# Falling rows of the second batch's short chunk: loaded row by row into two halves of a tile, with one on-chip copy in place of two

## The chip, the cores and the metric

The kernel runs on one core of a Trainium2 chip. The core has four compute engines that work side by side: TensorE (PE, matrix products; its weight loads are listed as PEld), VectorE (DVE), ScalarE (ACT) and GpSimd (POOL). SyncE (SP) computes nothing here; it issues transfers, and 16 DMA engines carry them out. The metric is the device time of one execution in microseconds (us), the median of several runs.

## The reference

The input x has 8 batches of 3008 rows of 256 numbers. The reference takes the real part of a two-dimensional Fourier transform of each batch and sends every row through a gated layer of 1536 hidden units:

```python
X = np.fft.fft(x, axis=1)
X = np.fft.fft(X, axis=2)
x = X.real.reshape(24064, 256)
g = x @ w_gate
silu = g * (1.0 / (1.0 + np.exp(-g)))
out = (silu * (x @ w_val)) @ w_out
```

## The kernel before

The Fourier transform is done by matrix products with tables of cosines and sines. Because of its symmetries the rows of a batch are first added and subtracted against one another ("folded"): a row that rises through the batch meets a row that falls through it. Each batch is loaded in two chunks: a long one, tile XA (128 partitions), and a short one, tile XC, of NCR = 60 rows. XC is laid out as partitions x 8 groups x 2 rows x 256: groups 0 to 3 hold the rising rows, groups 4 to 7 the falling ones, and each load brings two neighbouring rows side by side (2 KB), so the third index is the row's parity. Odd batches lie in partitions 64 to 123. Where two batches share a fold, they do so by their halves of the tile; the second batch (b = 1) is folded alone, in one pass over all 128 partitions, and for that its other parity has to stand in partitions 0 to 59.

`load_c` (L152) gives the list of loads of a short chunk. For the second batch it has 22 entries: 15 rising loads (L160; 4 partitions each, 32 KB), 4 falling loads (L162; 60 partitions, 120 KB each), one row for the middle (L164), and the two copies within XC (L158; 240 KB each): the first brings the rising rows' parity 0 from partitions 64 to 123 down to 0 to 59 (as parity 1), the second the falling rows' parity 1 (as parity 0). `fold_steps` (L171) makes the fold on POOL; its first operation is L178 (SDf from XC or XA), then L179, L182, L185 and so on. The partitions 60 to 63 and 124 to 127, which no load writes, are cleared once (L566) by two transfers from a tile of zeros; the zeros are a POOL memset (L563, on the space of Af), and `row_signs` (L345, L346, two small POOL operations) stands between that memset and the clears.

All loads, on-chip copies and output stores of the main part are issued by SP, so they stand in one queue, in program order. Around the change this queue holds: clears, C loads and copies of the second batch, its A loads (L148: 16 of 64 KB; L150: 4 of 256 KB), output stores (L1609), C loads of the third batch (L160, L162), and more stores.

The 24064 rows pass in tiles of 512 columns. For a tile PE makes g and v (L1335), ACT and DVE make from them the gated products (es L1470, sp L1447 and L1519, sv L1522 on ACT; sg L1451, sv L1538, hp L1549 on DVE), POOL makes hm from a pair's sv (L1546), PE multiplies by the last weights (o, L1597), ACT copies o to ev (L1603), and SP stores ev (L1609). There are two sv buffers, three for ev and two for es.

The order of all this after the prologue is made by a list scheduler when the program is built (`Sched`, L1130): each operation is entered by `S.add` with an engine, a duration, what it reads and writes, and for a load its share of the ring (`ring`) and its latency; `S.run` (L1995) starts from a time at which each engine comes free, and gives each engine its sequence. `run_loads` (L1658) enters the loads. What the scheduler is told of a load thus alters the order on every engine. `before` (L1893 to L1898) hangs small jobs on numbered units of the work; L1874 and L1875 are memsets of one of them (`halve_tables`).

Other lines that the steps touch: L356 (DVE) and L352 (POOL) prepare angles in the prologue, L677 to L679 (POOL) fold the first batch, L1818 (POOL) scales weights, L1969 issues Wo, the last weights, from POOL's own queue; L385 issued the weights before it. L660 and L634 are ACT operations of the prologue, L1373 (DVE) the product hp of the first, narrower tiles.

Of the kernel before, what the change touches and what calls it, by code (L numbers as in the profile page):

```python
# [31 lines left out]
def kernel(  # L32
# [8 lines left out]
    nc = tc.nc  # L41
    B, M, D = x.shape
    Dff = moe_w_gate.shape[1]
    P = 128
# [3 lines left out]
    R = M // 4  # L48
# [17 lines left out]
    NCR = GH - P  # L66
# [37 lines left out]
    zero = const.tile([P, 1], F32, name="zero")  # L104
# [6 lines left out]
    Z0 = const.tile([P, 2, 3, P], BF16, name="Z0")  # L111
# [5 lines left out]
    XC = const.tile([P, 8, 2, D], F32, name="XC")  # L117
# [14 lines left out]
    LC, NC_ = 4, NCR // 4  # L132

    def up_block(b, j, n):
        return rows_at(b, 2 * j - 1, [[2 * D, n], [R * D, 4], [1, 2 * D]])

    def rows_at(b, row, ap):
        return bass.AP(tensor=x.tensor, offset=(b * M + row) * D, ap=ap)

    def down_set(b, a, j, L, n):  # L140

        return rows_at(b, R * (a + 1) - 2 * j, [[2 * L * D, n], [-2 * D, L], [1, 2 * D]])

    JA, JC = P - LA + 1, GH - LC + 1
# [7 lines left out]
    def load_c(b, q):  # L152

        X3 = XC.rearrange("p a q d -> p a (q d)")
        p0 = 64 * (b % 2)
        pm = p0 + NCR
        r = slice(p0, p0 + NCR)
        half = [lambda s=s: q.dma_start(out=XC[0:NCR, 4 * s:4 * s + 4, 1 - s], in_=XC[r, 4 * s:4 * s + 4, s])  # L158
                for s in range(2)]
        return ([lambda h=h: q.dma_start(out=X3[p0 + LC * h:p0 + LC * (h + 1), 0:4, :],  # L160
                                         in_=up_block(b, JC - LC * h, LC)) for h in range(NC_)] +
                [lambda a=a: q.dma_start(out=X3[r, 4 + a, :], in_=down_set(b, a, JC, LC, NC_))  # L162
                 for a in range(4)] +
                [lambda: q.dma_start(out=XC[pm:pm + 1, 0:4, 1],  # L164
                                     in_=rows_at(b, 0, [[R * D, 1], [R * D, 4], [1, D]]))] +
                (half if b == 1 else []))

    def fold_steps(eng, X, CE, BB, q, r):  # L171
        tt = eng.tensor_tensor
# [74 lines left out]
    q = nc.sync  # L247
# [3 lines left out]
    zeros = Af.rearrange("p a b d -> p (a b d)")[:, 0:D]  # L251
# [51 lines left out]
    def col(name, n=1, dt=F32):  # L303
        small[name] = tp.tile([P, n], dt, name=name)
        return small[name]
# [17 lines left out]
    half, pc, inside = col("half"), col("pc"), col("inside")  # L323
# [20 lines left out]
    def row_signs():  # L344
        pts(sgo, pc, scalar1=float(NCR), scalar2=-2.0, op0=Alu.is_equal, op1=Alu.mult)  # L345
        pts(sgo, sgo, scalar1=1.0, scalar2=sgn, op0=Alu.add, op1=Alu.mult)  # L346
# [30 lines left out]
    def load_w(first, only=(0, 1)):  # L377
        for i, src in ((0, moe_w_gate), (1, moe_w_val)):
            if i not in only:
                continue  # L380
            w_ = src.rearrange("(no p) f -> p no f", p=P)
            if first:
                nc.gpsimd.dma_start(out=W0[i], in_=w_[:, :, 0:T])
            else:
                nc.gpsimd.dma_start(out=Wraw[i][:, :, 0:Dff - T], in_=w_[:, :, T:Dff])  # L385
# [11 lines left out]
                        in_=rows_at(0, 0, [[2 * R * D, 2], [R * D, 2], [1, D]]))  # L397
    pts(putC, putC, scalar1=pcol, scalar2=1.0, op0=Alu.is_equal, op1=Alu.mult)
    nc.gpsimd.memset(EOf[:, 1, :, P:P + 1], 0.0)
    nc.gpsimd.memset(sel[0:1, :], 1.0)  # L400
    nc.gpsimd.memset(Z0, 0.0)
    load_w(1, (0,))


# [71 lines left out]
    def set_cols(ps, tab, a):  # L476
        if a % 2:
            return (ps[:, 0:2 * GH + 2].rearrange("p (t n) -> p t n", t=2),
                    tab[:, 0:2 * NCE].rearrange("p (t n) -> p t n", t=2)[:, :, 0:GH + 1])
        return ps[:, 0:NCE], tab[:, 0:NCE]  # L480
# [7 lines left out]
    def folded_c(eo):  # L488
        for a in range(2):
            for q in range(2):  # L490
                dst, rhs = set_cols(acc[eo][q], Tab[:, 1, q, eo], a)
                nc.tensor.matmul(dst, EB[:, eo, a, q, :], rhs, start=False, stop=a == 1, skip_group_check=True)
# [64 lines left out]
    X3c = XC.rearrange("p a q d -> p (a q d)")  # L557
# [2 lines left out]
    heads(nc.gpsimd, hd[:, 0], hd[:, 1], CEa)  # L560
    heads(nc.gpsimd, SC[:, 0, 0, :, 0:1], SC[:, 0, 1, :, 0:1], CEc)
    nc.gpsimd.tensor_copy(EOA[:, 0, :, :, P:P + 1], SA[:, 0, :, :, 0:1])
    nc.gpsimd.memset(zeros, 0.0)  # L563
    row_signs()
    for hi in range(2):
        q.dma_start(out=X3c[64 * hi + NCR:64 * hi + 64, :].rearrange("p (c d) -> p c d", d=D),  # L566
                    in_=zeros[64 * hi + NCR:64 * hi + 64].unsqueeze(1).to_broadcast([64 - NCR, 16, D]))
    ptile, qtile = {}, {}

    def pq_tiles(t):  # L570
# [87 lines left out]
    first_tile = {(b, part): tile_of(b * H + part * 2 * G) for b, part in jobs}  # L658
    for k in range(2):
        nc.scalar.activation(BBc[:, :, 1, k, 0:1], SC[:, 0, 1 - k, :, 0:1], AF.Copy, scale=(nsgn, sgn)[k])  # L660
    folded_c(0)
    transform(0, 0, (0,), acc)
    for k in range(2):
# [673 lines left out]
    S = Sched()  # L1337
# [320 lines left out]
    def run_loads(n):  # L1658
        for what, k, fn in loads[:n]:
            up = k < (NA if what[0] == "A" else NC_)  # L1660
            r, w, us, ring = [], [((what[0],), k)], 0.4 if up else 0.62, 0.57 if up or what[0] == "C" else 1.14
            if what == ("A", 1):
                r = [(("C",), NC_ + 6)]
            if what[1] == 1:
                us, ring = 0.6, (0.6 if up else 0.9) if what[0] == "A" else 0.9 if up else 0.7
            if what == ("C", 1) and k > NC_ + 4:
                s = k - NC_ - 5
                r, w = [(("C",), j) for j in (range(NC_, NC_ + 4) if s else range(NC_))], [(("C",), k)]
            S.add("SP", us, fn, r=r, w=w, after=[(("A",), "pre" if k > 15 else "preW")] if what == ("A", 1) else [],
                  lat=2.5, ring=ring)  # L1670
        del loads[:n]
# [4 lines left out]
    def fold_step(what, i, unit):  # L1676
        kind, b = what
        q, j = (1, i) if what == ("C", 1) else divmod(i, 6)
        if i == 0:
            run_loads(max((k + 1 for k, (w_, _, _) in enumerate(loads) if w_ == what), default=0))  # L1680
# [27 lines left out]
    def load_next(what):  # L1708
        kind, b = what
        if kind == "A":  # L1710
            if b + 1 < B:
                loads.extend((("A", b + 1), k, fn) for k, fn in enumerate(load_a(b + 1, nc.sync)))
        else:
            b = b // 2 * 2 + 2
            if b < B:
                loads.extend((("C", b), k, fn) for k, fn in enumerate(load_c(b, nc.sync) + load_c(b + 1, nc.sync)))
# [173 lines left out]
    def odd_op(i):  # L1890
# [4 lines left out]
              7: [lambda: sine_op(0), rows_op], 8: [lambda: sine_op(1)], 9: [weigh_op],  # L1895
              13: [lambda: odd_op(0)], 14: [lambda: odd_op(1)], 15: [lambda: odd_op(2)], 16: [lambda: odd_op(3)],
              17: [lambda: S.add("POOL", 0.8, halve_tables, w=[(("Tab",), "z")])],
              6: []}  # L1898
    before.setdefault(SIGN_AT, []).append(signed_op)

    def row_width(t):
# [43 lines left out]
    for i, u in enumerate(units):  # L1945
# [4 lines left out]
        if i == 1:  # L1950
            loads.extend((("C", 1), k, fn) for k, fn in enumerate(load_c(1, nc.sync)))
        if i == A1_LOAD:
            loads[0:0] = ((("A", 1), k, fn) for k, fn in enumerate(load_a(1, nc.sync)))
        run_loads(LOADS if i < 20 else LOADS_LATER)
        if i in ROW_PE:
            row_op(ROW_PE[i])
# [7 lines left out]
        if i == RESCALE:  # L1964
            state["scaled"] = True
            S.add("ACT", 1.3, lambda: nc.scalar.activation(Wm[:, 1], Wm[:, 1], AF.Copy, scale=-0.5),
                  r=[(("Wm",), (fc, 1)) for fc in range(3)], w=[(("Wm",), 1)])
        if i == 2:
            S.add("POOL", 1.06, lambda: nc.gpsimd.dma_start(out=Wo, in_=moe_w_out.rearrange("(f p) d -> p f d", p=P)),  # L1969
                  w=[(("Wo",), 0)], lat=12.0)  # L1970
# [21 lines left out]
    part_b(prev)  # L1992
    owork = OWork(prev[0], ((psG, "g"), (psV, "v"), (psO, "o")))
    owork.run(len(owork.steps))
    S.run({'DVE': 1.2, 'ACT': 0.9, 'POOL': 4.7, 'PE': 0.0})  # L1995


# [28 lines left out]
```

## Time and profile before

| | us |
|---|---|
| median of 3 runs (604.05, 604.25, 605.38) | 604.25 |
| the profiled execution | 605.04 |
| its span in the profile | 603.2 |
| PE, DVE, ACT, POOL busy | 594.7, 573.2, 562.7, 510.5 |
| zeros' memset on POOL; clears issued | 17.49; 17.82 |
| rising, falling, middle loads of the second batch's C issued from | 19.36, 29.21, 34.68 |
| the two copies within XC issued | 37.84, 39.43 |
| XA's first load; folds of C and of A begin | 40.41; 44.17, 60.33 |

Times in a row of the profile's timeline are a start, counted from the beginning of the span, and a length. A row that stands for several instructions ("x15") runs from the first's start to the last's end. In square brackets stands how long the engine was idle before it and what released it. A row of SP is the issue of a transfer, not the transfer. Busy shares say how full an engine is over the whole span, not which of them sets the end; the chain of work that ended last, also by engine, says that. In the tables by stretches an engine that is busy for the whole length of the stretch has no slack in it.

### The profile page before, as it was taken

How to read it: one execution, taken by the hardware profiler on the slowest of the kernel's cores; microseconds unless marked ns; L12 is line 12 of the kernel's file. 1: busy time of each engine (PE TensorE's matmuls, PEld its weight loads, DVE VectorE, ACT ScalarE, POOL GpSimd, SP SyncE). 2: the span in 40 equal slices, each digit the busy share in tenths (PEclk: the TensorE clock that was granted, in tenths of full speed). 3: DMA queues.
4: the chain of work that ended last, by engine and by line, in shares of the span. 5: the costliest groups of instructions: out<-in, count | busy, mean ns of one | idle time of the engine just before them, and what ended most of it. 6: DMA issues, size and time to landing. Idle time of an engine off the chain costs nothing.

```text
span 603.2 us, 12562 instructions
## 1 busy us (share of the span) xinstructions
PE 594.7 (99%) x4031; PEld 392.2 (65%) x4031; DVE 573.2 (95%) x1055; ACT 562.7 (93%) x1085; POOL 510.5 (85%) x461
## 2 busy tenths in 40 slices
PE   9999999999999999999999999999999999999997
PEld 6556656665666666666666666666666666666686
DVE  8989999999999999999999999999999999999993
ACT  8899987899998999999999999999999999999994
POOL 8828999999799999998999988887878467687772
PEclk9999999999999999999999999999999999999999
DMA  9777346244716224454145212037211212111112
GB/s 239 125 130 137 106 119 202 80 132 121 177 37 168 80 64 127 110 143 122 48 85 143 62 50 77 18 91 184 63 62 37 62 39 69 38 55 51 54 53 79
DMA packets 50510, 57.90 MB, mean 96 GB/s; under 512 B 7222, under 2 KB 37114, under 8 KB 50444
## 3 DMA queue, kind: packets, MB, share of 16 engines
q1 hardware_dynamic: 47484, 54.22, 33.8%
q0 software_dynamic: 2672, 2.36, 2.7%
q8 instruction: 31, 0.51, 0.3%
q10 hardware_dynamic: 288, 0.52, 0.3%
q14 instruction: 35, 0.29, 0.2%
HBM read 29.43 MB, written 24.65 MB: 90 GB/s over the span
## 4 chain that ended last, share of the span: by engine, by line
PE 91%; ACT 4%; DMA 2%; issue 1%; POOL 1%; SPq 0%; DVE 0%; ACTq 0%; DVEq 0%
PE o L1597 39%; PE g L1335 26%; PE v L1335 19%; PE g L1755 2%; PE o L1755 2%; DMA XA<-in_x_dram 1%; PE v L1597 1%; ACT sv L1522 1%; DMA out_dram<-ev 1%; ACT sp L1447 1%; DMA XC<-in_x_dram 0%; ACT sg L1370 0%; POOL EOA L500 0%; ACT es L1470 0%; ACT v L1408 0%
## 5 line engine op out<-in xcount | busy, mean ns | idle before, releaser
L1546 POOL TENSOR_TENSOR hm<-sv 128x1024 bf16<-128x1024 f32 (+2 forms) x137 | 255.2, 1864 | 53.7 <-ACT sv L1522 27.6
L1538 DVE SCALAR_TENSOR_TENSOR sv<-es,v 128x512 f32<-128x512 f32 (+2 forms) x264 | 175.7, 669 | 6.2 <-PE v L1335 5.2
L1597 PE MATMUL o<-Wo,hm 128*128 128x256 bf16 (+1 forms) x1128 | 164.0, 272 | 0.0
L1549 DVE TENSOR_TENSOR hp<-sp,v 128x512 bf16<-128x512 f32 (+2 forms) x238 | 157.8, 670 | 4.6 <-PE v L1335 3.9
L1597 PE MATMUL o<-Wo,hp 128*128 128x256 bf16 (+1 forms) x1104 | 160.1, 272 | 0.0
L1597 PEld LDWEIGHTS <-hm 128*128 128x128 bf16 (+2 forms) x1140 | 111.7, 98 | 59.0 <-issue 2.2
L1597 PEld LDWEIGHTS <-hp 128*128 128x128 bf16 (+2 forms) x1140 | 111.9, 98 | 56.1 <-issue 1.9
L1522 ACT ACTIVATE sv<-g 128x512 f32<-128x512 f32 (+2 forms) x182 | 121.3, 681 | 3.0 <-PE g L1335 2.7
L1447 ACT ACTIVATE sp<-g 128x512 f32<-128x512 f32 (+2 forms) x182 | 113.2, 627 | 4.7 <-PE g L1335 2.7
L1335 PE MATMUL g<-Pt,Wp 128*128 128x512 bf16 (+2 forms) x288 | 107.8, 374 | 1.0 <-ACT sp L1519 0.7
L1408 ACT ACTIVATE v<-bc,w 128x512 f32<-128x512 bf16 (+2 forms) x146 | 105.7, 726 | 2.0 <-DVE sv L1538 0.9
L1335 PE MATMUL g<-Qt,Wq 128*128 128x512 bf16 (+2 forms) x288 | 105.9, 375 | 0.0
L1335 PE MATMUL v<-Pt,Wp 128*128 128x512 bf16 (+2 forms) x288 | 105.6, 375 | 0.0
L1472 DVE SCALAR_TENSOR_TENSOR es<-bc,w,v 128x512 f32<-128x512 bf16 (+2 forms) x128 | 93.2, 732 | 3.2 <-PE v L1335 0.8
L1470 ACT ACTIVATE es<-v 128x512 f32<-128x512 f32 (+2 forms) x146 | 90.7, 624 | 5.4 <-PE v L1335 2.4
L1335 PEld LDWEIGHTS <-Wp 128*128 128x128 bf16 x576 | 56.3, 98 | 27.4 <-issue 3.0
L1335 PE MATMUL g<-Qt,Wm 128*128 128x512 bf16 (+2 forms) x196 | 73.3, 376 | 0.1
L1451 DVE SCALAR_TENSOR_TENSOR sg<-bc,w,g 128x512 f32<-128x512 bf16 (+2 forms) x92 | 66.2, 722 | 1.4 <-PE g L1335 1.0
L1522 ACT ACTIVATE sv<-sg 128x512 f32<-128x512 f32 (+2 forms) x92 | 64.3, 703 | 1.0 <-DVE sg L1515 0.9
L1335 PE MATMUL v<-Qt,Wm 128*128 128x512 bf16 (+2 forms) x160 | 59.8, 374 | 1.9 <-ACT es L1470 1.2
L1519 ACT ACTIVATE sp<-g 128x512 f32<-128x512 f32 (+2 forms) x92 | 57.1, 620 | 4.8 <-DVE sg L1515 4.6
L1515 DVE SCALAR_TENSOR_TENSOR sg<-sg,g 128x512 f32<-128x512 f32 (+2 forms) x92 | 60.7, 660 | 0.3 <-PE g L1335 0.2
(196 smaller groups left out, 757.1 us busy)
## 6 DMA issues: line engine op xcount, KB each, us to landing
out_dram<-ev SPq DMA_DIRECT2D x96, 128.0 KB
XA<-in_x_dram SPq DMA_DIRECT2D x30, 256.0 KB
XA<-in_x_dram SPq DMA_DIRECT2D x112, 64.0 KB
XC<-in_x_dram SPq DMA_DIRECT2D x32, 120.0 KB
XC<-in_x_dram SPq DMA_DIRECT2D x105, 32.0 KB
bc<-br SPq DMA_DIRECT2D x19, 128.0 KB
St<-Fc SPq DMA_DIRECT2D x12, 128.5 KB
out_dram<-ev SPq DMA_DIRECT2D x12, 120.0 KB
```

Source lines behind the costliest of these rows:

```text
L1335: nc.tensor.matmul(ps[:, :n], Wt[:, gv, fs], src[:, :n], start=start, stop=stop, skip_group_check=True)
L1408: nc.scalar.activation(T_[kv][:, :w], bc[t][:, :w], AF.Copy, scale=w0[:, 1, f:f + 1])
L1447: nc.scalar.activation(sp_to()[:, :w], T_[kg][:, :w], AF.Silu)
L1451: nc.vector.scalar_tensor_tensor(T_[keg][:, :w], bc[t][:, :w], w0[:, 0, f:f + 1], T_[kg][:, :w], op0=Alu.mult, op1=Alu.add)
L1470: nc.scalar.activation(T_[kes][:, :w], T_[kv][:, :w], AF.Copy, scale=2.0 if on_pool(u) > 1 else 1.0)
L1472: nc.vector.scalar_tensor_tensor(T_[kes][:, :w], bc[t][:, :w], w0[:, 1, f:f + 1], T_[kv][:, :w], op0=Alu.mult, op1=Alu.add)
L1515: nc.vector.scalar_tensor_tensor(T_[kgm][:, :w], T_[keg][:, :w], 2.0, T_[kg][:, :w], op0=Alu.mult, op1=Alu.subtract)
L1522: nc.scalar.activation(sv()[:, f % 2, w - 1::-1, 1], T_[kgm if by_dve else kg][:, :w], AF.Silu)
L1538: nc.vector.scalar_tensor_tensor(sv()[:, f % 2, w - 1::-1, 0], T_[kes][:, :w], 2.0, T_[kv][:, :w], op0=Alu.mult, op1=Alu.subtract)
L1546: nc.gpsimd.tensor_tensor(hts_(t)[1][:, f - 1:f + 1, :w], sv()[:, :, :w, 1], sv()[:, :, :w, 0], op=Alu.mult)
L1549: nc.vector.tensor_tensor(hts_(t)[0][:, f, :wp], T_[ksp][:, :wp], T_[kv][:, :wp], op=Alu.mult)
L1597: nc.tensor.matmul(st["ps"][:n, j, :], hts[t][minus][:, f, c:c + n], Wo[:, f, :], start=(f == 0), stop=(f == nF - 1))
```

## The change

The falling rows of the second batch's short chunk are no longer loaded in pairs. Each of the four groups is loaded twice, one row of 1 KB per partition: parity 0 to partitions 64 to 123, parity 1 straight to partitions 0 to 59. So the second copy within XC is gone; the copy of the rising rows stays. The list has 25 entries: the middle row, 15 rising loads, 4 falling loads of parity 0, the copy, 4 falling loads of parity 1. The other batches load as before.

The zeros for the clears are now made by ACT (a copy of a broadcast zero) behind L660, and the clears are issued there. `row_signs` moves earlier on POOL, to where Z0 was cleared, and Z0's memset becomes a job of unit 18. The costs of these loads for the scheduler and the beginnings of POOL and SP are changed with it, and XA's loads now stand behind entry 24 of the list in place of entry 21.

```diff
-        half = [lambda s=s: q.dma_start(out=XC[0:NCR, 4 * s:4 * s + 4, 1 - s], in_=XC[r, 4 * s:4 * s + 4, s])
-                for s in range(2)]
...
+        def down(a, k):
+            q.dma_start(out=XC[0:NCR, 4 + a, 0] if k else XC[r, 4 + a, 0],
+                        in_=rows_at(b, R * (a + 1) - 2 * JC + k, [[2 * LC * D, NC_], [-2 * D, LC], [1, D]]))
+
+        downs = [[lambda a=a, k=k: down(a, k) for a in range(4)] for k in range(2)]
+        return mid + ups + downs[0] + [lambda: q.dma_start(out=XC[0:NCR, 0:4, 1], in_=XC[r, 0:4, 0])] + downs[1]
...
-    nc.gpsimd.memset(Z0, 0.0)
+    row_signs()
     load_w(1, (0,))
...
-    nc.gpsimd.memset(zeros, 0.0)
-    row_signs()
-    for hi in range(2):
-        q.dma_start(out=X3c[64 * hi + NCR:64 * hi + 64, :].rearrange("p (c d) -> p c d", d=D),
-                    in_=zeros[64 * hi + NCR:64 * hi + 64].unsqueeze(1).to_broadcast([64 - NCR, 16, D]))
...
         nc.scalar.activation(BBc[:, :, 1, k, 0:1], SC[:, 0, 1 - k, :, 0:1], AF.Copy, scale=(nsgn, sgn)[k])
+    nc.scalar.copy(zeros, zero.to_broadcast([P, D]))
+    for hi in range(2):
+        q.dma_start(out=X3c[64 * hi + NCR:64 * hi + 64, :].rearrange("p (c d) -> p c d", d=D),
+                    in_=zeros[64 * hi + NCR:64 * hi + 64].unsqueeze(1).to_broadcast([64 - NCR, 16, D]))
...
             if what == ("A", 1):
-                r = [(("C",), NC_ + 6)]
-            if what[1] == 1:
-                us, ring = 0.6, (0.6 if up else 0.9) if what[0] == "A" else 0.9 if up else 0.7
-            if what == ("C", 1) and k > NC_ + 4:
-                s = k - NC_ - 5
-                r, w = [(("C",), j) for j in (range(NC_, NC_ + 4) if s else range(NC_))], [(("C",), k)]
+                r = [(("C",), NC_ + 9)]
+                us, ring = 0.6, 0.6 if up else 0.9
+            if what == ("C", 1):
+                us, ring = (0.6, 0.6) if k <= NC_ else (0.9, 0.9)
+                if k == NC_ + 5:
+                    r = [(("C",), j) for j in range(1, NC_ + 1)]
...
-              6: []}
+              18: [lambda: S.add("POOL", 0.8, lambda: nc.gpsimd.memset(Z0, 0.0), w=[(("Z0",), k) for k in range(2)])]}
...
-    S.run({'DVE': 1.2, 'ACT': 0.9, 'POOL': 4.7, 'PE': 0.0})
+    S.run({'DVE': 1.2, 'ACT': 0.9, 'POOL': 3.5, 'PE': 0.0, 'SP': -2.0})
```

More of the change, by code (lines that the diff above doesn't have):

```diff
@@ L157, in load_c @@
         r = slice(p0, p0 + NCR)
-        half = [lambda s=s: q.dma_start(out=XC[0:NCR, 4 * s:4 * s + 4, 1 - s], in_=XC[r, 4 * s:4 * s + 4, s])
-                for s in range(2)]
[L160 to L166, printed above, removed]
+        ups = [lambda h=h: q.dma_start(out=X3[p0 + LC * h:p0 + LC * (h + 1), 0:4, :],
+                                       in_=up_block(b, JC - LC * h, LC)) for h in range(NC_)]
+        mid = [lambda: q.dma_start(out=XC[pm:pm + 1, 0:4, 1],
+                                   in_=rows_at(b, 0, [[R * D, 1], [R * D, 4], [1, D]]))]
+        if b != 1:
+            return ups + [lambda a=a: q.dma_start(out=X3[r, 4 + a, :], in_=down_set(b, a, JC, LC, NC_))
+                          for a in range(4)] + mid
+        def down(a, k):
[3 more added lines that the diff above has]
+        return mid + ups + downs[0] + [lambda: q.dma_start(out=XC[0:NCR, 0:4, 1], in_=XC[r, 0:4, 0])] + downs[1]
     def fold_steps(eng, X, CE, BB, q, r):
```

## The prediction

> **What bounds the kernel now.** I read the page first (busy shares, chain by engine), then busy time by stretches, then the queue of SP and the rows of POOL, DVE and ACT around the places where PE stands still.
>
> ```profile
> span 603.2 us, 12562 instructions
> PE 594.7 (99%) x4031; PEld 392.2 (65%) x4031; DVE 573.2 (95%) x1055; ACT 562.7 (93%) x1085; POOL 510.5 (85%) x461
> PE 91%; ACT 4%; DMA 2%; issue 1%; POOL 1%; SPq 0%; DVE 0%; ACTq 0%; DVEq 0%
> ```
>
> PE is the bound, so an edit counts by what it adds to, or takes from, the few places where PE waits. By stretches (columns: length; then PE, PEld, DVE, ACT, POOL busy with counts; granted clock, DMA share, GB/s):
>
> ```profile
> 60.00:70.00 10.00, 10.00 (x69) 6.81 (x68) 9.88 (x17) 10.00 (x21) 9.89 (x8) 1.00 0.35 109
> 70.00:82.00 12.00, 10.69 (x72) 6.87 (x71) 10.76 (x18) 10.51 (x21) 11.92 (x13) 1.00 0.39 104
> 82.00:155.00 73.00, 72.26 (x495) 48.03 (x493) 70.17 (x131) 64.36 (x126) 71.33 (x70) 1.00 0.48 132
> ```
>
> Just after the changed loads, at 60 to 70, PE, DVE, ACT and POOL are all full: a delay of one there can't be made up. PE's loss is at 70 to 82. Its place, in PE's, ACT's and the chain's rows:
>
> ```profile
> 79.75 0.38 PE L1335 MATMUL v<-Qt,Wm 128*128 128x512 bf16 x1 [1.20 <-ACT es L1470]
> ...
> 78.61 0.59 ACT L1603 COPY ev<-o 128x512 f32<-128x512 f32 x1 [1.49 <-PE o L1597]
> ...
> 74.48 0.56 SPq L1609
> 75.09 3.37 DMA out_dram<-ev
> ```
>
> The page names o as the releaser of that ACT copy, but the chain names the store issued at 74.48, whose transfer ends at 78.5: the copy waits for an ev buffer. Its contents were written at 60.73, and the store left 13.8 us later because SP's queue was full of loads. PE loses here 1.63 (gaps of 1.36 and 0.27 between 77.9 and 80.2). The changed loads stand in this queue:
>
> ```profile
> 17.82 1.50 SPq L566 DMA_DIRECT2D XC<-Af  x2
> 19.36 9.69 SPq L160 DMA_DIRECT2D XC<-in_x_dram  x15
> 29.21 5.29 SPq L162 DMA_DIRECT2D XC<-in_x_dram  x4
> 34.68 0.65 SPq L164 DMA_DIRECT2D XC<-in_x_dram  x1
> 37.84 2.47 SPq L158 DMA_DIRECT2D XC<-XC  x2
> 40.41 9.74 SPq L148 DMA_DIRECT2D XA<-in_x_dram  x16
> ...
> 66.17 3.66 SPq L162 DMA_DIRECT2D XC<-in_x_dram  x4
> ```
>
> Each row's length is from its first issue to its last. And POOL, whose order the change rewrites:
>
> ```profile
> 58.33 1.90 POOL L1546 TENSOR_TENSOR hm<-sv 128x1024 bf16<-128x1024 f32 x1 [2.61 <-ACT sv L1522]
> 60.33 2.36 POOL L178 TENSOR_TENSOR SDf<-XA 128x1020 f32<-128x1020 f32 x1
> 62.64 0.23 POOL L179 TENSOR_TENSOR EOf<-XA 128x4 f32<-128x4 f32 x1
> 62.80 1.91 POOL L1546 TENSOR_TENSOR hm<-sv 128x1024 bf16<-128x1024 f32 x1
> ...
> 62.06 0.68 DVE L1538 SCALAR_TENSOR_TENSOR sv<-es,v 128x512 f32<-128x512 f32 x1
> ```
>
> POOL stands idle 2.61 us, does hm of one pair of tiles, then the fold of XA; the last part of the last XA load signals at 60.2 in the trace's completion records, just before the fold. There are two sv buffers: DVE's sv at 62.06 writes the one that hm at 58.33 has read.
>
> **The change, part by part.**
>
> *Zeros and clears.* The zeros' memset (17.49) and the two sign operations leave POOL ahead of the IOTA at 18.47, so POOL is 18.47 - 17.49 = 0.98 earlier, down to Wo's issue at 25.23. ACT gains one 128x256 copy, about 0.26, into the 0.27 that it idles before L634 at 16.64: nothing; without that cover 0.26. SP's queue has been idle for 8.9 before the clears, so their issue goes with their gate from 17.82 to about 16.7, behind the copy's end at 16.6. The sign operations (0.25 + 0.26) now stand where Z0's memset (0.73) stood at about 7 us, so POOL loses nothing there. The Z0 memset (0.73, the row of L1875) moves behind 33.68, where POOL is idle until 44.17: nothing; without cover 0.73.
>
> *When the 15 rising loads are down.* Copy 1 waits for them (37.84). By the completion records they land one after another, #1 at 26.5 to #8 at 29.2, 0.35 to 0.4 apart, then #9 at 31.6 to #15 at 37.8, about 1.1 apart, while Wo's weights (issued 25.23, landed 38.4) pass through the same DMA engines. If the rising loads start d earlier and Wo e earlier, #15 lands (1.1/0.35) d - (1.1/0.35 - 1) e = 3.1 d - 2.1 e earlier. Both parts move about 1.0, so the two nearly cancel. Ends: d = 1.1 and e = 0.6 give 2.2 earlier (POOL loses part of its 0.98 to VectorE); d = 0.5 and e = 0.9 give 0.4 later (the clears gain little, since the weights fill the engines, as the rows by queue show: packets, MB, share of the 16 engines):
>
> ```profile
> q0 software_dynamic: 452, 0.89, 108.3%
> ```
>
> That is 17.0 to 21.5: no packet of SP's queue although the first clear was issued at 17.82. I take 0.6 earlier, near the middle: copy 1 at 37.2. The middle row's move to the front (0.65 of issue) lies in this wait.
>
> *Between copy 1 and the XA loads.* SP issues 25 loads and copies in place of 22. Before: copy 1 at 37.84, XA's first load at 40.41, 2.57. After, one copy (0.89) and then four falling loads of parity 1, which write the lower half (the copy's rows are the rising ones, so they need not wait for it); they are issued back to back as those of the third batch are, 3.66 for four, and 0.1 of gaps: 4.65. The first four falling loads (60 KB instead of 120) still stand ahead of the copy, in its wait. The second copy's 240 KB are gone. Balance for XA's loads: -0.6 + 4.65 - 2.57 = +1.5; call it D. Ends: -2.2 + 2.08 = -0.1, and +0.4 + 2.08 = +2.5. The loads from 40.41 on are limited by landing, so D reaches the last of them: XA is down at 60.2 + 1.5 = 61.7.
>
> *POOL's order.* The list scheduler is told that these loads are cheaper (rising 0.6 for 0.9 on the ring, SP beginning 2.0 sooner), and it puts the fold of XA (L178, L179) ahead of the hm that ran at 58.33. So POOL, idle from 55.7, now waits for XA, and hm is queued behind: fold 61.75, hm at 61.75 + 2.31 + 0.16 = 64.2, done 66.1. DVE's sv (62.06) and ACT's sv behind it wait for that: 4.05 late. DVE is busy 9.88 + 10.76 of the 22 us from 60 to 82, so it can make up 1.36; ACT 1.49. The wait for the store at 78.5 lies in this idle time: ACT comes to it about 2.5 late, the store at the same time or 1.5 later, and PE's 1.63 goes into the new stall. Net for PE: 4.05 less 1.36 to 1.63, about +2.5. POOL (21.8 of 22 busy) comes out up to 4 late and finds 1.7 idle in 82 to 155; its hm at 83.22 ends 85.1, and DVE reuses that buffer about 0.9 later, so up to 1 more: kept in the range.
>
> *The rest.* DVE's, ACT's and PE's orders differ from about 82 to 155 and are the same after it. The 0.74 PE loses there (73.00 - 72.26) could go, or a stall like it could come: 0, with ends of -0.7 and +1. VectorE's two L356 operations at 21.02 took 1.62 and 0.56 where the same pair at 27.00 took 1.27 together; the long one lies beside POOL's L677. With POOL 1 earlier two of POOL's may meet them: +0.5 at PE's wait for hp at 23.82, which the 62 us stall then takes up, since everything ahead of XA's landing has slack there.
>
> Sum: 605.04 + 2.5 = 607.5 for the profiled execution (span 603.2 and 1.8 around it). That run stands 0.8 above the median of 604.25; against the median 606.7.
>
> **The rivals.**
> 1. *XA comes early (faster).* If XA is down by 57.7, the fold fills POOL's 2.61 idle, hm ends by 62.06 and nobody waits. That is 2.5 earlier than 60.2: XA's loads from 37.9, copy 1 at 33.3, 4.5 earlier than now. Then the stores at 74 leave 2.5 earlier too and land before 77: PE's 1.63 goes. Against it the 0.5 of L356 now counts: -1.1 to -1.6, 602.6 to 603.2. For it: d = 1.5 with e = 0 would give 4.6, and the clears may use the weights' time. Against: the row of 17.0 to 21.5, and Wo moving too. 21%. [...]
> 2. *It cancels.* Copy 1 about 2 earlier, D near 0: POOL's stall is 60.1 - 57.7 = 2.4 at most, taken up by the 1.63 and the other slack: 604.2 to 605.2. 13%.
> 3. *A larger stall.* D at 2.5 gives 5.05 late, +3.5, and with POOL's lateness +1: 607.8 to 609. It is the upper part of my own case.
>
> **How the numbers follow.** My case, XA late and hm behind it, has 66%, from 605.6 to 609.0. It is over 0.2% (1.2 us, about what can be told from no change) above 604.25. Rival 1 has 21%, of it 1% within 0.2%; rival 2 has 13%. So faster 0.20, same 0.14, slower 0.66. For eight in ten the range must take in some of rival 1: 602.9 to 609.0, half of rival 1's chance and the ends above 609 left out.
>
> **What would show it.** Right: copy 1 issued at 36.5 to 38, XA's first load later than 40.41, POOL idle some 6 us before SDf<-XA at 61 to 62.5, hm after it, DVE and ACT waiting at 62 to 66 for hm, no ACT wait for ev at 78. Wrong: XA's first load by 37.9 and the fold at about 56 to 58; or the hm ahead of DVE's sv ended in time for another reason. L356's pair shows its term by its own row.

## The result and the profile after

The changed kernel takes 608.05 us (median of 6 runs, 606.54 to 608.48); the kernel before took 604.70 beside it. The ratio is 1.0049, interval 1.0033 to 1.0065: slower by half a per cent. Its profiled execution took 608.12, span 606.3. A second set of the same kernel gave 608.00, ratio 1.0060 (1.0035 to 1.0085).

Busy time by stretches of the changed kernel (length; PE, PEld, DVE, ACT, POOL busy with counts; granted clock, DMA share, GB/s):

```profile
60.00:70.00 10.00, 6.99 (x37) 4.16 (x36) 5.84 (x10) 6.63 (x14) 7.92 (x6) 0.83 0.40 122
70.00:82.00 12.00, 11.95 (x84) 8.32 (x84) 11.31 (x19) 11.74 (x24) 11.92 (x12) 1.00 0.40 108
82.00:155.00 73.00, 71.91 (x485) 47.80 (x490) 70.30 (x127) 63.50 (x126) 71.44 (x68) 1.00 0.49 129
```

The four engines that were full from 60 to 70 all have a hole there now, and the granted clock of that stretch is 0.83. From 70 to 82 PE's old loss is gone. From SP's queue:

```profile
16.58 1.49 SPq L660 DMA_DIRECT2D XC<-Af  x2
26.11 0.64 SPq L160 DMA_DIRECT2D XC<-in_x_dram  x1
26.80 8.16 SPq L158 DMA_DIRECT2D XC<-in_x_dram  x15
35.16 3.62 SPq L167 DMA_DIRECT2D XC<-in_x_dram  x4
38.97 0.89 SPq L171 DMA_DIRECT2D XC<-XC  x1
39.90 3.49 SPq L167 DMA_DIRECT2D XC<-in_x_dram  x4
43.56 8.52 SPq L148 DMA_DIRECT2D XA<-in_x_dram  x16
```

Between the clears and the middle row (L160) the queue stands still for 8 us. The waits of SP say for what (us, times, longest):

```profile
SPq L160 <- DMA XC<-Af: 8.0, 1, 8.0
```

and so does the chain of that stretch (a start, a length, what):

```profile
17.39 8.70 DMA XC<-Af
26.11 4.95 DMA XC<-in_x_dram
```

The middle row goes into partition 124, which the clears write too, so it waits until they have landed, and the 15 rising loads wait behind it. POOL, DVE and PE where the loss is made:

```profile
62.08 2.35 POOL L180 TENSOR_TENSOR SDf<-XA 128x1020 f32<-128x1020 f32 x1 [5.05 <-DMA out_dram<-ev]
64.39 0.21 POOL L181 TENSOR_TENSOR EOf<-XA 128x4 f32<-128x4 f32 x1
64.54 1.89 POOL L1547 TENSOR_TENSOR hm<-sv 128x1024 bf16<-128x1024 f32 x1
...
66.47 0.69 DVE L1539 SCALAR_TENSOR_TENSOR sv<-es,v 128x512 f32<-128x512 f32 x1 [4.05 <-POOL hm L1547]
...
67.16 0.58 PE L1336 MATMUL g<-Pt,Wp 128*128 128x512 bf16 x1 [2.94 <-ACT sv L1523]
67.54 0.63 PE L1336 MATMUL g<-Qt,Wq 128*128 128x512 bf16 x1
...
70.51 0.38 PE L1336 MATMUL g<-Pt,Wp 128*128 128x512 bf16 x1
```

POOL waits for XA. The row names a store (out_dram<-ev) as the releaser, but the fold reads no ev, and in the trace's completion records the last part of XA's last load signals at 61.78, just before the fold. hm is behind the fold, DVE waits 4.05 for hm, and PE stands still for 2.94. The matmuls after PE's gap last 0.6 instead of 0.38, for about 3 us. Where the time is lost is seen by the starts of the weight loads in the two traces, matched by their number (4031 in each), after less before:

| weight load | before | after | difference |
|---|---|---|---|
| 387, first after PE's gap | 63.74 | 67.16 | 3.42 |
| 400, clock back | 65.69 | 70.51 | 4.82 |
| 489, behind the old wait for ev | 80.23 | 83.32 | 3.09 |
| 800, between the orders that differ | 125.77 | 128.88 | 3.11 |
| 4000 | 595.60 | 598.57 | 2.97 |

About 0.3 stood there before the gap. It came up by 16 us, after VectorE had waited 0.61 for a load of the first batch, and the second trace of the changed kernel was 0.41 ahead at 17 us instead: it is a difference between executions. So: +0.3, +3.1 for the gap, +1.4 for the slow matmuls, -1.7 for the ev wait that is gone, and nothing from 82 to the end.

### The profile page after: what moved, and what is told of

Read it like the earlier page. It is cut to its first block, busy times and chain, and to the rows that moved or that the text cites. A ratio compares the mean times of both kernels' runs of the same rounds, so it can differ in the third digit from the quotient of the medians.

```text
span 606.3 us, 12501 instructions
## 1 busy us (share of the span) xinstructions
PE 592.3 (98%) x3974; PEld 391.8 (65%) x4031; DVE 572.3 (94%) x1055; ACT 562.1 (93%) x1086; POOL 509.7 (84%) x460
## 4 chain that ended last, share of the span: by engine, by line
PE 82%; DMA 6%; DVE 4%; SPq 2%; ACT 2%; issue 2%; POOL 1%; ACTq 0%; DVEq 0%
PE o L1598 37%; PE g L1336 22%; PE v L1336 18%; DMA XC<-in_x_dram 2%; PE g L1756 2%; DMA XA<-in_x_dram 2%; PE o L1756 2%; DMA XC<-Af 1%; DVE sv L1539 1%; SPq L167 1%; DMA out_dram<-ev 1%; PE v L1598 1%; DVE hp L1550 1%; POOL EOA L502 0%; DVE SA L444 0%
## 5 line engine op out<-in xcount | busy, mean ns | idle before, releaser
L1336 PE MATMUL g<-Pt,Wp 128*128 128x512 bf16 (+2 forms) x281 | 105.4, 375 | 4.0 <-ACT sv L1523 2.9
L1336 PE MATMUL g<-Qt,Wq 128*128 128x512 bf16 (+2 forms) x249 | 91.5, 375 | 0.4
L1452 DVE SCALAR_TENSOR_TENSOR sg<-bc,w,g 128x512 f32<-128x512 bf16 (+2 forms) x92 | 66.1, 721 | 1.4 <-PE g L1336 1.0
L1336 PEld LDWEIGHTS <-Wq 128*128 128x128 bf16 x430 | 42.0, 98 | 31.5 <-issue 7.1
```

Source lines behind the costliest of these rows:

```text
L1336: nc.tensor.matmul(ps[:, :n], Wt[:, gv, fs], src[:, :n], start=start, stop=stop, skip_group_check=True)
L1452: nc.vector.scalar_tensor_tensor(T_[keg][:, :w], bc[t][:, :w], w0[:, 0, f:f + 1], T_[kg][:, :w], op0=Alu.mult, op1=Alu.add)
```

## The experiments

Medians, ratio to the kernel before on the same chip with its interval, start of XA's fold on POOL, PE's gap between 62 and 70, and the granted clock of 60 to 70 in the profiled execution:

| kernel | us | ratio (interval) | XA's fold | gap | clock |
|---|---|---|---|---|---|
| changed, again | 608.00 | 1.0060 (1.0035-1.0085) | 61.63 | 2.49 | 0.83 |
| fold_behind | 607.34 | 1.0047 (1.0033-1.0062) | 61.41 | none | 1.00 |
| fold_late | 606.73 | 1.0031 (1.0015-1.0048) | 63.49 | none | 1.00 |
| fold_ahead | 605.46 | 1.0015 (1.0004-1.0026) | 60.10 | 1.34 | 1.00 |
| mid_behind | 607.93 | 1.0045 (1.0026-1.0063) | 62.26 | 3.18 | 0.85 |
| act_zeros | 604.49 | 0.9997 (0.9987-1.0007) | 60.11 | none | 1.00 |
| old_falls | 607.29 | 1.0040 (1.0025-1.0055) | 61.78 | 3.15 | 0.84 |
| wide | 603.14 | 0.9978 (0.9968-0.9988) | 54.49 | none | 1.00 |
| wide_before | 604.06 | 1.0002 (0.9993-1.0011) | 60.08 | none | 1.00 |
| stores_early | 604.24 | 1.0000 (0.9989-1.0010) | 61.34 | none | 1.00 |
| lead | 604.26 | 0.9989 (0.9976-1.0003) | 57.48 | none | 1.00 |
| lead_behind | 604.09 | 0.9996 (0.9987-1.0004) | 59.95 | none | 1.00 |

In all of them the sequence of every other engine is that of the kernel that they come from; only what the diff names is moved. The first row is the changed kernel once more:

> The changed kernel itself once more, as a measure of how far XA's landing and the loss differ from run to run on one chip. XA's fold between 60.5 and 63.5, VectorE's wait for hm 2.5 to 5.5 us, granted clock under 1.00 in the 10 us after it if TensorE's gap is near 3 us again: 606.5 to 609.

It did as expected; its fold of XA began 0.45 earlier than in the first trace and PE's gap was 0.45 shorter, with the clock down as before. One of its seven runs took 612.37; no trace shows why.

### What POOL's order does: fold_ahead, fold_behind, fold_late

fold_ahead moves one step in the kernel before, when the scheduler's list is ready:

```diff
...
+            fold, hm1 = pool[k], pool[k - 1]
+            order.remove(fold)
+            order.insert(order.index(hm1), fold)
```

> The kernel before with one thing changed: on POOL the fold of XA stands ahead of the hm that ran at 58.33, everything else as before. XA lands at 60.2 as before, so hm ends at 60.3 + 2.5 + 1.85 = 64.6 and VectorE's sv of 62.06 starts 2.6 later. If the order on POOL is the cause: TensorE loses 1.5 to 2 us near 64, the wait of 1.63 us for ev near 78 goes, net between 0 and +0.7, so 604.3 to 605.5; the clock stays at 1.00 if a gap of 1.5 us is too short to lower it (the gap of 1.36 us in the kernel before lowered nothing). If the clock falls after any such gap, about 1.4 us more, 606 to 607. If the loads are the cause and not the order: no change from before.

POOL of fold_ahead:

```profile
60.10 2.35 POOL L178 TENSOR_TENSOR SDf<-XA 128x1020 f32<-128x1020 f32 x1 [4.15 <-DMA out_dram<-ev]
62.41 0.22 POOL L179 TENSOR_TENSOR EOf<-XA 128x4 f32<-128x4 f32 x1
62.56 3.75 POOL L1554 TENSOR_TENSOR hm<-sv 128x1024 bf16<-128x1024 f32 x2
```

605.46, inside what was expected if the order is a cause. PE's gap of 1.34 leaves the clock at 1.00. So the order alone costs 0.15% even where the loads come as early as before.

fold_behind puts the order back in the changed kernel, fold_late goes one hm further:

```diff
 fold_behind
...
+            fold, hm1, nxt, hm2 = pool[k:k + 4]
+            order.remove(fold)
+            order.insert(order.index(hm1) + 1, fold)
+            order.remove(nxt)
+            order.insert(order.index(hm2) + 1, nxt)
 fold_late
...
+            for o, to in ((fold, hm2), (s1, hm3), (s2, s1)):
+                order.remove(o)
+                order.insert(order.index(to) + 1, o)
```

> The changed kernel with one thing put back: on POOL the fold of XA stands behind the hm that it had been put ahead of (and the next fold step behind the next hm), every other engine's order and all loads as changed. If the loss is made by POOL's order: XA still lands at about 62.0, but hm runs at about 58 to 60, VectorE's 4.05 us wait for hm goes, TensorE's gap of 2.94 us at 64 to 67 goes, and with it the slow matmuls after it (granted clock back to 1.00); the wait for an ev buffer near 78 comes back, about 1 us longer than before since the stores leave 1.1 later: 605 to 606. If the later loads themselves cost the time (SP's queue, stores late), or the new orders between 82 and 155 us do: it stays at 607.5 to 608.3.

> The changed kernel with POOL's order alone altered, further than in fold_behind: the fold of XA stands behind the next two hm (the two fold steps after it behind the third), so that no hm that is due before about 66 us stands behind XA's landing. Loads, queue and every other order as changed. fold_behind gave 605.5 in its profiled execution but 607.3 as a median, and its second hm still stood behind the fold: if XA lands at different times from run to run (61 to 63) and the loss is hm's waiting for it, this one loses nothing there in any run: 604.5 to 606, with a narrow spread, and no slow matmuls. If the median of fold_behind came from something else in the changed kernel (the prologue, the orders from 82 to 155 us, the ev stores), this stays at 607 or more.

The first fell between the two theories: PE's gap and the slow clock went, and the profiled execution took 605.5, but the five other runs took 607.3 to 609.0. What those runs looked like no trace shows; four of the five have a granted clock of 0.999 or 1.000 over the whole execution (0.997 in the changed kernel's profiled one), so a slow stage of TensorE does not explain them. fold_late missed as well: in its trace no hm waits for XA and no matmul is slow, and still it took 606.73, in the profiled execution too. Its runs were expected close together and lie between 605.11 and 608.56. Its waits between 50 and 90 (engine, line, waited for: us, times, longest):

```profile
ACT ev L1611 <- DMA out_dram<-ev: 2.0, 1, 2.0
PE v L1343 <- ACT es L1478: 1.7, 1, 1.7
ACT sp L1455 <- POOL hp L1563: 1.0, 1, 1.0
```

The late loads are paid in other places: the stores leave later, so the old wait for ev is 2.0 instead of 1.5, and the second batch's short chunk is folded later, so that POOL's hp, which stands behind that fold, comes 1.0 late. PE is 0.6 behind there and another 0.5 near 78. The order on POOL turns the late loads into one large stall, but without that order most of the loss stays: the ratio is 1.0047 and 1.0031 with late loads alone, 1.0015 with the order alone, and 1.0049 and 1.0060 with both.

### When the loads land: wide, wide_before

```diff
+        if b == 1:
+            ups = [lambda a=a: q.dma_start(out=X3[r, a, :],
+                                           in_=rows_at(b, R * a + 2 * (JC - LC * NC_ + LC) - 1, [[2 * D, NCR], [1, 2 * D]]))
+                   for a in range(4)] + [lambda: None] * (NC_ - 4)
... (wide alone)
-        return mid + ups + downs[0] + ...
+        return ups + mid + downs[0] + ...
```

Both kernels load the same rows in another order, so the second batch's part of the output is permuted and is not the reference's: they measure time alone.

> A probe of the rival in which XA comes early: the changed kernel, with POOL's new order, but the second batch's 15 rising loads of 4 partitions replaced by 4 loads over 60 partitions of the same rows in another order (so that batch's values are permuted and its part of the output is not the reference's), and the middle row behind them. By the prediction's threshold (copy by 33.3, XA's loads from 37.9, XA down by 57.7): four loads of 60 partitions issue in 3.7 us and land before 30, the copy leaves by 31, XA's loads start by 36 and XA is down by 57; the fold then fills POOL's idle time, neither VectorE's wait at 62 nor the wait for ev near 78 is there: 602.3 to 603.3. If the change's order costs time also when XA is early: 605 or more.

> The same four wide rising loads in the kernel before (POOL's old order, two copies; the second batch's values are permuted in the same way). XA early changes nothing on POOL there, where hm stands first; the ev stores leave earlier, so the 1.63 us near 78 goes: 602.6 to 603.4. With the probe wide it shows what POOL's new order is worth when XA is early: by my reading nothing or up to 0.5 us.

SP and POOL of wide:

```profile
31.34 0.89 SPq L175 DMA_DIRECT2D XC<-XC  x1
32.28 3.49 SPq L171 DMA_DIRECT2D XC<-in_x_dram  x4
35.95 8.90 SPq L148 DMA_DIRECT2D XA<-in_x_dram  x16
...
53.25 1.28 POOL L1560 TENSOR_TENSOR hp<-sp,pp 128x512 bf16<-128x512 f32 x1
54.49 2.36 POOL L184 TENSOR_TENSOR SDf<-XA 128x1020 f32<-128x1020 f32 x1
56.80 0.21 POOL L185 TENSOR_TENSOR EOf<-XA 128x4 f32<-128x4 f32 x1
58.36 1.90 POOL L1551 TENSOR_TENSOR hm<-sv 128x1024 bf16<-128x1024 f32 x1 [1.35 <-ACT sv L1527]
```

With the copy at 31.34 and XA's loads from 35.95 the fold lies in POOL's idle time, hm starts at 58.36 as in the kernel before, and the time is 603.14 (all runs 602.89 to 603.38): the number that the first rival gave. wide has the changed kernel's order on POOL, PE, DVE and ACT. So the 4.9 us between it and the changed kernel (608.00 to 608.05) come from the way the rising loads and the middle row are issued, and none from the new orders where XA is early. wide_before was expected no later than 603.4 and took 604.06: by the medians the rest of the change is worth 0.9 with early loads, although the two profiled executions took 603.19 and 603.24. A possible reason is in stores_early.

### Which part of the queue: mid_behind, old_falls, act_zeros, lead

```diff
 mid_behind
-        return mid + ups + downs[0] + ...
+        return ups + mid + downs[0] + ...
 old_falls
-        return mid + ups + downs[0] + [copy] + downs[1]
...
+        return mid + ups + pairs + half + [lambda: None] * 3
```

> The changed kernel with one load moved: the middle row (into partition 124, which the clears write) behind the 15 rising loads instead of ahead of them; all other engines' orders are the same. In the changed kernel SP waits for the clears to land before it issues it (17.4 to 26.1), and the rising loads wait behind. If that wait is what made copy and XA late: the rising loads are issued from 18.1, and the copy by 37 or earlier instead of 38.97, XA's last load lands at 60 or earlier instead of 62.0, and the time falls by 1.5 or more, to 606.5 or less; if they get so far ahead of Wo that the copy leaves by 33.3, the stall goes wholly: 602.5 to 603.5. If the rising loads are held by the DMA engines in any case (15 loads landing one by one until 37.8, as before): the copy moves by 1 at most and the time by 1 at most, 607 to 608.

> The changed kernel with the one thing in its name undone: the falling rows are loaded in pairs again (4 loads of 120 KB) and both copies are there, the middle row still in front, all other orders as changed. Copy 1 at about 39, copy 2 about 1.1 later, XA's first load at 41.4 instead of 43.56, XA down 1 to 2 earlier, at 60 to 61. By my theory (every us of XA's landing between 57.7 and 62 costs about one): 1 to 2 us less than the changed kernel, 606 to 607.2. If the parity loads don't matter: 607.5 to 608.3.

SP and POOL of mid_behind:

```profile
36.59 0.89 SPq L171 DMA_DIRECT2D XC<-XC  x1
...
41.67 9.40 SPq L148 DMA_DIRECT2D XA<-in_x_dram  x16
...
62.26 2.35 POOL L180 TENSOR_TENSOR SDf<-XA 128x1020 f32<-128x1020 f32 x1 [7.40 <-DMA out_dram<-ev]
```

mid_behind's copy went to 36.59 and XA's first load to 41.67, as expected of the wait, but XA came down no earlier (62.26), since its loads took longer (20.59 from the first issue to the fold, 18.52 in the changed kernel), and the median is 607.93 where 606.5 or less was expected. So the middle row's wait alone does not make the loss. Its runs lie between 603.85 and 609.85, the widest of all. old_falls, which undoes the edit that the change is named for, has XA's first load at 41.44, 2.1 earlier than the changed kernel, and its fold still at 61.78, where 60 to 61 was expected. It gains 0.7 on the changed kernel timed beside it, less than the intervals can tell apart: loading by parity alone is not what costs either. Why XA lands at about 62 in both, though its loads start 2 us earlier, is open.

act_zeros is the kernel before with the zeros on ACT, the sign operations and the Z0 memset moved:

> The kernel before with the zeros made by ScalarE, the sign operations and Z0's memset moved and the clears issued at about 16.6 as in the change; loads, copies and every other order as before. By the prediction's rule 3.1 d - 2.1 e with both about 1: copy 1 issued about 0.6 earlier than 37.84 (0.4 later to 2.2 earlier), XA lands about 0.6 earlier, time within 0.5 of before, 603.8 to 604.8; VectorE's first L356 pair 0.3 to 0.5 later. If the clears use turns inside the weights' time: copy 1 at 35 or earlier and the ev wait near 78 shorter, 603 to 603.5.

Copy 1 left at 36.82, 1.0 earlier, and the median is the same, as expected: hm, which stands first on POOL, ended at 60.1 as before. Its profiled execution, however, took 603.63. Busy time from 70 to 82 there, and the three stores:

```profile
70.00:82.00 12.00, 12.00 (x82) 7.91 (x81) 11.65 (x20) 11.59 (x23) 11.92 (x13) 1.00 0.37 105
...
73.39 1.15 SPq L1610 DMA_DIRECT2D out_dram<-ev  x3
```

The stores left 0.7 earlier than in the trace of before (74.10), ACT's wait for ev fell from 1.5 to 0.2, and PE lost nothing near 78. In this execution 0.7 was enough to remove that wait. The eleven runs lie between 602.98 and 605.40; how many of them have the wait no trace shows.

lead keeps the changed kernel's parts and reorders SP's queue alone, with one small clear split off to go first ([copy] stands for the copy within XC, clears for the rest of the two clears):

```diff
-    for hi in range(2):
-        q.dma_start(out=..., in_=zeros[...])
+    q.dma_start(out=X3c[NCR:64, 0:D], in_=zeros[NCR:64])
...
-        return mid + ups + downs[0] + [copy] + downs[1]
+        return ups + clears + downs[0] + [copy] + downs[1] + mid
```

> The changed kernel with SP's queue alone in another order, the result kept: one small clear of 4 partitions x 1 KB as the gate, then the 15 rising loads, then the rest of the clears, the falling loads, the copy and last the middle row. In the changed kernel the two clears of 64 KB and the wait of the middle row for them (17.4 to 26.1) stand ahead of the rising loads. If their place in the queue is what makes XA late: rising loads issued from 17 and landing 3 us or more ahead of where they did, so that more of them pass before Wo's transfer; copy by 34, XA's first load by 39, XA down by 58, no wait for hm: 602.9 to 604. If the rising loads push the weights back instead, TensorE waits near 21 to 25 for them (1 us or more): 604 to 605.5. If the queue's order doesn't matter: 607 to 608.

SP and POOL of lead:

```profile
16.39 0.69 SPq L666 DMA_DIRECT2D XC<-Af  x1
17.12 8.95 SPq L160 DMA_DIRECT2D XC<-in_x_dram  x15
26.11 1.41 SPq L671 DMA_DIRECT2D XC<-Af  x2
...
33.68 0.88 SPq L178 DMA_DIRECT2D XC<-XC  x1
...
39.60 8.14 SPq L148 DMA_DIRECT2D XA<-in_x_dram  x16
...
57.48 2.35 POOL L187 TENSOR_TENSOR SDf<-XA 128x1020 f32<-128x1020 f32 x1 [3.01 <-DMA out_dram<-ev]
```

The copy leaves 5.3 earlier than in the changed kernel, XA's fold starts at 57.48, no hm is waited for, and 3.7 of the 4.9 us are back. The median is 0.26 above what was expected. In its profiled execution (604.33) PE is 1.62 ahead of the kernel before at weight load 489, as in wide (1.60); it then lost 0.7 between 394 and 423 us, where ACT waited 0.8 for a transfer to bc, far from the loads. lead_behind adds POOL's old order, so that a later XA does no harm:

> The queue order of lead together with POOL's order of fold_behind: rising loads ahead of the clears and the middle row last, and the fold of XA behind the hm that it had been put ahead of. lead had most runs at 603.4 to 604.4 and three of twelve at 605.5 to 606.4. If those three are runs in which XA landed later than 57.7 and hm waited for it: with hm first, XA may land as late as 60.3 at no cost, and they go, 603.0 to 604.0, below the kernel before by 0.1% to 0.25%. If they have another cause (the L358 pair meeting POOL's operations, weights late): the same spread as lead, about 604.2.

604.09, just above what was expected if late XA was the reason of lead's longest runs, and near the 604.2 of the other case. Two of the twelve runs still took 605.20 and 605.29 (three took 605.50 to 606.40 in lead), so what makes them is open. The ratio to the kernel before is 0.9996 (0.9987 to 1.0004). Neither version beats the kernel before by more than can be measured.

### The other stall: stores_early

The kernel before, with three stores moved forward in SP's sequence:

```diff
...
+            for n, o in enumerate(sp[74:77]):
+                order.remove(o)
+                order.insert(order.index(sp[59 if n == 0 else 73 + n]) + 1, o)
```

> The kernel before with three stores of one ev buffer (those issued at 74.10 to 75.5) moved on SP's queue right behind the three stores issued at 63.91; all else as before. If ScalarE's copy at 78.6 waits for that store, as the chain says, and not for TensorE's o: the wait goes and TensorE's 1.63 us with it, 602.6 to 603.4. If it waits for o: no change, 604.3 to 605. The loads behind the stores go 1.2 us later, which costs nothing that the trace shows.

The wait for ev near 78 went, so the copy did wait for the store, as the chain said, and not for o: PE is busy for all of 70 to 82, and its place against the kernel before falls from +1.19 to -0.44 there, 1.63 in all. The time did not follow, since this execution had lost 1.2 at 23.8. DVE of stores_early:

```profile
21.14 3.27 DVE L356 SCALAR_TENSOR_TENSOR XA<-XA,mM 128x376 f32<-128x376 f32 x2
```

The same pair took 2.18 in the trace shown of before. It is the pair that meets POOL's two operations on BBa: here they started at 21.19 and 22.43, and both halves of the pair were long, 1.73 beside the first and 1.62 beside the second; in the trace of before the halves took 0.63 and 1.62. In the ten traces in which POOL is 1 us earlier the pair took 2.19 to 2.52; in the four with POOL's old place 2.18 or 2.19 three times and 3.27 once. In the kernel before the later wait for ev would hide it: whatever PE loses at 24, it waits less at 78. That fits wide against wide_before (0.9) and the one run of stores_early at 602.74 among ten at 603.9 to 604.7, but for the runs without a trace it is argued and not shown. Why a half is long beside POOL's operations no run shows.

## Why the prediction was right, and where not

The direction and the mechanism came out, and the size roughly: 608.05 against 606.7, within the range and within the likeliest case's own (605.6 to 609.0). For the profiled execution it was 608.12 against 607.5; the 0.8 that the working took off for the median did not show. That the sums came so close is in part luck, since two pairs of errors cancelled. By its steps:

- *POOL's order, XA late, hm behind it.* Fold at 61.75 forecast, 62.08 measured; hm done at 66.1 and 66.4; DVE's sv 4.05 late forecast, 4.41 late measured (66.47 against 62.06), 4.05 of it idle. fold_ahead shows that the order costs by itself. But fold_late shows that the late loads cost more than half of the loss without it: "one stall" was too simple.
- *"The middle row's move to the front lies in this wait."* Wrong. It was costed at 0.65 of issue; it waits for the clears, in the same partition, until 26.11, and the 15 rising loads behind it are issued from 26.80 instead of 19.36. The bound of 0.4 later for the copy was too narrow: 38.97, 1.13 later. XA's first load was 3.15 later, beyond the end of 2.5 given to D. What this step costs in time is not shown: mid_behind, which undoes it, has the copy at 36.59 and is no faster.
- *"D reaches the last of them."* Wrong, in the other direction: 3.15 at the first load, 1.8 at the fold, since the 16 rising loads of XA were issued in 8.52 instead of 9.74. The two errors cancelled by luck to 0.3.
- *The balance of PE.* 4.05 less 1.36 to 1.63 was to give +2.5. Measured: a gap of 3.1, not 4.05 (PE had about 1 us of work ready), 1.7 back near 78, and 1.4 for the slow matmuls, which the working did not have at all. The gap taken too large and the slow matmuls left out cancelled too, so that the profiled execution's +3.1 stands near the +2.5.
- *L356.* The 0.5 on the pair did not show: it took 2.19, and 2.18 before. With POOL earlier no trace has the 3.27 of stores_early, but one case among four traces is too few to say that the earlier POOL prevents it.
- *The reorder from 82 to 155*, 0 with ends of -0.7 and +1: 3.09 at its beginning, 2.97 at the end.
- *The clears inside the weights.* Issued 1.24 earlier they landed no earlier: the loads that waited for them went at 26.11, and at 26.25 in the kernel before, after this wait:

```profile
SPq L160 <- DMA XC<-Af: 1.0, 1, 1.0
```

From 17.0 to 21.5 the changed kernel's trace has 443 packets of q0, the weights' queue, and 3 of q1, SP's (107.4% and 0.2% of the 16 engines), although the clears were issued from 16.58. So the first rival's premise, that the clears may use the weights' time, fell, as the row of 17.0 to 21.5 had it.
- *The first rival's arithmetic* held where its condition was made true: 602.6 to 603.2 forecast for an early XA, 603.14 measured in wide. lead, whose fold at 57.48 also meets the condition, had 604.26.

## What to carry to other kernels

A load moved ahead in a queue takes its own waits with it: look which earlier transfer writes the same partitions before costing the move at its issue, because all that stands behind it waits too (8.0 here, with 15 loads behind it). Then look whether the work that needs the data comes earlier at all: moving XA's first load by 2 us did not move its landing in mid_behind and old_falls. A scheduler that is told of cheaper loads can put work that needs them ahead of work that does not (which of the edited costs did it here no run separates); on POOL, with hm behind the fold, this turned a late load into a stall of the whole chain (DVE idle 4.05, PE 2.94), so check such a step by the landing and not by the issue. And a stall of one engine can hide another's: taking one away (the stores, 1.63) may only uncover the one before it (1.2 in the trace of stores_early).

## What the runs showed of the hardware

TensorE's clock fell after its gap: gaps of 2.94, 2.49, 3.18 and 3.15 us (the changed kernel, again, mid_behind, old_falls) were followed by about 3 us of matmuls at 0.57 to 0.63 instead of 0.38 (granted clock 0.83 to 0.85 in that stretch of 10, and 0.50 from 66.7 to 70.0 in the changed kernel's trace), a gap of 1.34 (fold_ahead) by none: its clock stayed at 1.00. In the changed kernel that cost 1.4 on top of the gap's 3.1.
